# The first superblock's second product from seven products of halves, list-scheduled, with the low parts of w_out kept in SBUF

## The chip, the cores and the metric

The kernel runs on one core of a Trainium2 chip. The metric is the device time of one execution in microseconds. Engines are named as in the profile: PE (TensorE), PEld (its weight loads), DVE (VectorE), ACT (ScalarE), POOL (GpSimd), SP (SyncE, whose queue issues nearly all DMAs).

## The reference

Attention within chunks of 64 tokens, and behind it a feed-forward layer with ELU, all in float32:

```
scores = q @ k.T / 8              # 8 batches, 8 heads, 576 tokens in 9 chunks, head size 64
x      = softmax(scores) @ v      # -> 4608 tokens x 512
g      = elu(x @ w_in)            # 512 -> 2048
out    = g @ w_out                # 2048 -> 512
```

## The kernel before

**Split operands.** A float32 operand is held as a high part in PE's fast 32-bit format and a low part, the rest. `three` (L425 to L434) makes a product of two such operands from three matmuls (high with high, high with low, low with high) of 128 x 128 weights against 512 columns. All these matmuls have line 434.

**Blocks.** The 4608 tokens are 9 blocks of 512. Three plain blocks come first: for each of 16 slices f of the hidden layer, `hidden` makes h (12 matmuls), `elu` turns it into g, split into ghi and glo, and the second product adds g times w_out to four banks o0 to o3 (12 matmuls per f). `queue` holds the second products; they run one or two slices behind, and when the third block ends, 24 of these matmuls (f = 14 and 15) are left over.

**Superblocks.** The other six blocks are three pairs, "superblock" 0, 1 and 2. Two blocks are taken as a 2 x 2 arrangement of halves, and seven products of half size take the place of eight (`PRODUCTS`, `FIRST`, `SECOND`), with sums and differences of the operands made beforehand. A product over two blocks is 384 matmuls in the plain form and 336 in that of seven products.

- *First product.* The sums of w_in (`combine`) are made by POOL during the second block and written to `a_dram`. The sums of x ("t1" to "t4") and their splits ("B11", "T2" and so on, `prepare`) are made as soon as the tiles of x are there.
- *Second product.* Its operands come from w_out: `Sums` takes a pair j of slices (there are 8 pairs), adds high and low part ("a", "b"), makes four differences ("c", "d"), casts the high part on ACT ("e"), makes the low part ("f") and writes four halves to `w_dram` ("g" to "j"); `write_raw` writes the parts that need no sum.
- *Superblocks 1 and 2* have both products in this form. `superblock` and `tokens` put every step with its reads, writes and a place in time into a `Plan`; `Plan.order` lists them with a table of costs per engine, which sets the order on each engine. First operands and w_out operands come through a ring of four places of 512 KB in SBUF, tile `ring` (`ring_slot`, `load_entry`), one entry for two steps of six matmuls each.
- *Superblock 0* has the first product of seven, written out by hand (`FIRST_PAIR`, `SECOND_PAIR`, `PAIR`): one pair g of hidden slices at a time, its seven operands loaded by `load_a` into the former place of w_in. Its second product is plain: one block beside the first products, the other from g kept in SBUF (`KEPT`). Since x operands take the place of w_out's low part, that low part is written to `lo_dram` in the first block (`write_lo`) and read back through a ring of four (`load_lo`).

**Attention.** A tile is 128 tokens. Its queries and keys are loaded as tokens, transposed on DVE, multiplied (`score`, L248), turned into probabilities, transposed in 32 x 32 blocks, copied by ACT (`unturned`, L393), swapped by four DMAs on SP's queue (`turned`, L399), and multiplied by v (`times_v`, L256). The softmax has two forms: one subtraction and one ACTIVATE for all (L362, L367) in the hand-written stages, eight ACTIVATEs by head (L1566) in the planned ones.

**Order.** PE, ACT, DVE and SP run in the order in which the program is written, up to the third block also POOL by the framework's order; strings such as `THIRD_BLOCK` are lists of items, one per instruction group. Each engine works its queue in order, so a waiting instruction holds what stands behind it.

## Time and profile before

| | |
|---|---|
| time, 3 runs | 829.26, 825.13, 828.77 us; median 828.77 |
| the profiled execution | 825.15 us, span 823.4 us |
| busy, share of the span | PE 98%, PEld 80%, DVE 74%, ACT 64%, POOL 21% |
| DMA | 191.90 MB, mean 233 GB/s |
| third block ends, superblock 0 begins | 319.3 us |
| superblock 1 begins | 499.4 us |
| superblock 2 begins | 665.0 us |

The page cuts the span in 40 slices and gives busy tenths per engine; the chain of waits follows the last instruction back to what released it. A matmul's duration in the timeline (0.39 us) is longer than the distance to the next (0.23 us), because matmuls overlap.

### The profile page before, as it was taken

How to read it: one execution, taken by the hardware profiler on the slowest of the kernel's cores; microseconds unless marked ns; L12 is line 12 of the kernel's file. 1: busy time of each engine (PE TensorE's matmuls, PEld its weight loads, DVE VectorE, ACT ScalarE, POOL GpSimd, SP SyncE). 2: the span in 40 equal slices, each digit the busy share in tenths (PEclk: the TensorE clock that was granted, in tenths of full speed). 3: DMA queues.
4: the chain of work that ended last, by engine and by line, in shares of the span. 5: the costliest groups of instructions: out<-in, count | busy, mean ns of one | idle time of the engine just before them, and what ended most of it. 6: DMA issues, size and time to landing. Idle time of an engine off the chain costs nothing.

```text
span 823.4 us, 15851 instructions
## 1 busy us (share of the span) xinstructions
PE 804.4 (98%) x5853; PEld 655.6 (80%) x5853; DVE 613.1 (74%) x914; ACT 523.5 (64%) x990; POOL 171.1 (21%) x149
## 2 busy tenths in 40 slices
PE   6799999999999999999999999999999999999997
PEld 5688878888778878878888888778788888888885
DVE  4999997666776659767656867868889956557964
ACT  5999885544554546766666445888867737776451
POOL 0000014264525531443111254000020100000100
PEclk9999999999999999999999999999999999999999
DMA  9976994889778887689986789999876585566755
GB/s 234 272 212 209 270 328 130 244 243 267 219 215 231 231 269 205 202 241 281 283 235 188 218 246 299 286 322 287 249 204 206 195 269 193 193 196 190 226 186 149
DMA packets 183229, 191.90 MB, mean 233 GB/s; under 512 B 84720, under 2 KB 151792, under 8 KB 183152
## 3 DMA queue, kind: packets, MB, share of 16 engines
q1 hardware_dynamic: 182512, 188.80, 77.2%
q0 software_dynamic: 640, 2.10, 0.6%
q8 instruction: 46, 0.75, 0.4%
q14 instruction: 31, 0.25, 0.1%
HBM read 144.18 MB, written 42.99 MB: 227 GB/s over the span
## 4 chain that ended last, share of the span: by engine, by line
PE 83%; DMA 8%; SPq 3%; ACT 2%; DVE 2%; issue 1%; DVEq 0%; ACTq 0%
PE o L434 43%; PE h L434 34%; DMA ring<-a_dram 3%; PE ps_a L248 2%; PE ps_a L256 2%; SPq L206 2%; PE h L451 1%; DMA st<-in_moe_w_out_dram 1%; DMA kept<-in_k_dram 1%; DMA a_dram<-wi_lo 1%; DMA kept<-in_q_dram 1%; DMA a_dram<-wi_hi 1%; DMA v_sb<-in_v_dram 1%; PE ps_a L315 1%; DMA ring<-w_dram 1%
## 5 line engine op out<-in xcount | busy, mean ns | idle before, releaser
L434 PE MATMUL o<-wo_hi,ghi 128*128 128x512 f32 x272 | 107.6, 396 | 0.0
L434 PE MATMUL o<-wo_hi,glo 128*128 128x512 f32 x272 | 106.1, 390 | 0.3 <-DVE glo L479 0.3
L434 PE MATMUL o<-wo_lo,ghi 128*128 128x512 f32 x272 | 106.0, 390 | 0.0
L434 PE MATMUL h<-xhi,wi_hi 128*128 128x512 f32 x228 | 84.0, 397 | 0.1
L434 PE MATMUL h<-xlo,wi_hi 128*128 128x512 f32 x228 | 82.3, 390 | 0.0
L434 PE MATMUL h<-xhi,wi_lo 128*128 128x512 f32 x180 | 70.3, 390 | 0.0
L434 PEld LDWEIGHTS o<-wo_hi,glo 128*128 128x128 f32 x272 | 51.1, 188 | 11.7 <-DVE glo L479 0.7
L434 PEld LDWEIGHTS o<-wo_hi,ghi 128*128 128x128 f32 x272 | 51.0, 188 | 11.1
L434 PEld LDWEIGHTS o<-wo_lo,ghi 128*128 128x128 f32 x272 | 51.1, 188 | 10.2
L510 POOL TENSOR_TENSOR kept<-wi_hi,wi_lo 128x512 f32<-128x512 f32 x16 | 21.7, 1376 | 158.8 <-DVE xf L172 118.2
L471 DVE SCALAR_TENSOR_TENSOR e<-e,h 128x512 f32<-128x512 f32 x48 | 32.8, 684 | 25.2 <-ACT e L469 24.8
L434 PE MATMUL o<-split,ring 128*128 128x512 f32 x216 | 51.0, 390 | 0.0
L434 PEld LDWEIGHTS h<-xhi,wi_hi 128*128 128x128 f32 x228 | 42.6, 188 | 9.8 <-ACT kept L785 0.8
L434 PEld LDWEIGHTS h<-xlo,wi_hi 128*128 128x128 f32 x228 | 42.8, 188 | 8.5
L434 PEld LDWEIGHTS o<-split,ring 128*128 128x128 f32 x216 | 40.5, 188 | 8.4
L393 ACT COPY unturned<-turned 128x512 f32<-128x512 f32 x28 | 17.4, 621 | 46.0 <-DVE turned L388 37.9
L468 ACT ACTIVATE e<-h 128x512 f32<-128x512 f32 x48 | 28.6, 596 | 25.0 <-PE h L434 22.5
L476 ACT CAST ghi<-e 128x512 fp32r<-128x512 f32 x48 | 29.8, 621 | 19.8 <-DVE e L471 19.6
L746 POOL TENSOR_TENSOR glo<-e,ghi 128x512 fp32r<-128x512 f32 x16 | 20.7, 1296 | 96.9 <-ACT ghi L744 96.9
L434 PE MATMUL h<-split,ring 128*128 128x512 f32 x168 | 40.3, 391 | 0.0
L1492 ACT ACTIVATE e<-e 128x512 f32<-128x512 f32 x64 | 39.5, 630 | 1.0
L434 PEld LDWEIGHTS h<-xhi,wi_lo 128*128 128x128 f32 x180 | 33.8, 188 | 7.5 <-DVE wi_lo L185 0.4
(225 smaller groups left out, 2011.3 us busy)
## 6 DMA issues: line engine op xcount, KB each, us to landing
ring<-a_dram SPq DMA_DIRECT2D x56, 512.0 KB, 5.3
ring<-w_dram SPq DMA_DIRECT2D x56, 512.0 KB, 4.3
wi_hi<-a_dram SPq DMA_DIRECT2D x56, 256.0 KB, 5.3
kept<-in_q_dram SPq DMA_DIRECT2D x100, 128.0 KB, 3.8
kept<-in_k_dram SPq DMA_DIRECT2D x100, 128.0 KB, 4.0
wo_lo<-lo_dram SPq DMA_DIRECT2D x20, 512.0 KB, 5.8
v_sb<-in_v_dram SPq DMA_DIRECT2D x32, 256.0 KB, 5.4
st<-in_moe_w_in_dram SPq DMA_DIRECT2D x16, 512.0 KB, 4.9
```

The costliest lines, as they stand in the source:

```text
L206: nc.sync.dma_start(out=dst[p0:p0 + n], in_=src[b, :, s0:s0 + n, :].rearrange("h s d -> s h d"))
L248: nc.tensor.matmul(scores[halves[c], j, hp, :], lhsT=qT[halves[j], hp, halves[c]], rhs=kT[halves[j], hp, halves[c]], start=True, stop=True,)
L256: nc.tensor.matmul(x_ps[halves[j], c, hp, :], lhsT=v_sb[halves[c], 2 * hp + j, :], rhs=aT[halves[c], :, j * NK + hp], start=True, stop=True,)
L315: nc.tensor.matmul(turned_ps[half, h, :], lhsT=a[half, h, :], rhs=ident[half, half], start=True, stop=True,)
L393: nc.scalar.copy(out=unturned, in_=turned)
L434: nc.tensor.matmul(ps, lhsT=a, rhs=b, start=start, stop=stop, skip_group_check=onto)
L468: nc.scalar.activation(out=e, in_=h, func=AF.Relu, scale=-1.0)
L471: nc.vector.scalar_tensor_tensor(out=e, in0=e, scalar=-1.0, in1=h, op0=ALU.add, op1=ALU.max)
L476: nc.scalar.copy(out=ghi, in_=e)
L510: nc.gpsimd.tensor_tensor(out=out, in0=a, in1=b, op=op)
L746: engine.tensor_tensor(out=lo, in0=e, in1=hi.bitcast(F32), op=ALU.subtract)
L1492: nc.scalar.activation(out=units[u], in_=units[u], func=AF.Exp, scale=-1.0)
```

## The change

- Superblock 0 goes through the same plan as 1 and 2: `FIRST_PAIR`, `PAIR`, `KEPT`, class `Pair` and their helpers are gone, and `for s in range(NS)` takes the place of `range(1, NS)`. Its second product is also of seven products, 336 matmuls for 384.
- The 24 leftover matmuls of the third block are planned ahead of its first step (at -1 to -0.35), and so are the rest of the x sums and the softmax of the first tile (at -1.5), whose v product comes at step 5.
- The low parts of w_out stay in SBUF: `lo_dram`, `write_lo` and `load_lo` are gone; T1 and T2 take the place of the first half's low part, and g of pairs 4 and 5 that of the second half's.
- The sums of w_out are spread anew: pair 0 in the second block on DVE, 1 and 2 on POOL and 3 on DVE in the third block, 4 to 7 in superblock 0's first phase (`LATE_SUMS`, begun at steps 0, 8, 16 and 24). Before, 4 and 5 were made in the third block, 0, 3 and 1 in superblock 0, and 2, 6 and 7 in superblock 1.
- The raw parts are all written by the end of the second block; the ring's first four entries are loaded from slice 9 of the third block on ("R0" to "R3").

The core of the diff:

```diff
-            early_sums[j] = Sums(j, sums_place(j), [weights[j // 4 if preparing == "third" else 0][3][
-                :, (2 * j + i) % (NF // 2), :] for i in range(2)])
+            early_sums[j] = Sums(j, kept_st[2][:, :4 * TB] if j == 3 else flat(io), lows_of(j))
...
-            sums.write_half(lo, half, nc.gpsimd if preparing == "third" else nc.sync)
+            sums.write_half(*divmod("ghij".index(part), 2), nc.sync if j in SUMS_ON_VECTOR else nc.gpsimd)
+
+    def lows_of(j: int):
+        return [w_out_slices(2 * j + i)[1] for i in range(2)]
...
-        both = flat((weights[0][1], weights[1][3], xhi, xlo, *t3_place)[place])[...
+        both = flat((weights[0][1], weights[0][3], xhi, xlo, *t3_place)[place])[...
...
-        wlo = w_out_slices(f)[1] if plain else weights[0][3][:, f % (NF // 2), :]
+        whi, wlo = w_out_slices(f)
...
-        14: "l H e q e xT1a k e e xt3a xt2a xT2a xt4a P",
-        15: "H s v e x V e xt1b xt3b xT1b e xt2b e xT2b xt4b",
+        14: "l H e q e xT1a k e e xt3a P",
+        15: "H s v e x V e e e",
...
-    SUMS_ON_VECTOR = (1,)
-    RAW_SECOND = {3: (3, 1), 6: (4, 1), 9: (5, 1)}
+    SUMS_ON_VECTOR = (0, 3)
+    RAW_SECOND = {2: (3, 1), 4: (3, 0), 6: (4, 1), 8: (4, 0), 10: (5, 1), 12: (5, 0)}
+    MORE_SECOND = {
+        4: "w0a w0b", 8: "w0c w0d", 9: "w0e", 12: "w0f", 13: "w0g w0h", 14: "w0i w0j",
+    }
     MORE_THIRD = {
-        2: "w4a", 3: "w4b", 4: "w4c w4d", 5: "w4e w4f", 6: "w4g w5a", 7: "w4h w5b", 8: "w4i w5c w5d", 9: "w4j w5e",
-        10: "w5f", 11: "w5g", 12: "w5h", 13: "w5i", 14: "w5j",
+        2: "w1a", 3: "w1b", 4: "w1c w1d", 5: "w1e w1f w3a", 6: "w1g w3b", 7: "w1h w3c w3d", 8: "w1i w3e w3f",
+        9: "w1j R0 w3g w2a", 10: "w2b w3h", 11: "R1 w3i w2c w2d", 12: "w3j w2e", 13: "R2 w2f w2g", 14: "w2h", 15: "R3 w2i w2j",
     }
...
-    LATE_SUMS = (2, 0), (6, 8), (7, 22)
+    LATE_SUMS = (4, 0, 2), (5, 8, 6), (6, 16, 7), (7, 24, 6)
...
-    SCORES = (5, 18, 31, 44, 57, 70, 83, 97)
+    SCORES = (5, 18, 31, 44, 56, 69, 82, 95)
...
+    for m, (name, cols) in enumerate((("t2", "a"), ("T2", "a"), ("t1", "b"), ("T1", "b"), ("t4", "a"), ("t3", "b"),
+                                      ("t2", "b"), ("T2", "b"), ("t4", "b"))):
+        add_prepare(-1.9 + .2 * m, name, cols)
+    for m, name in enumerate(("T3", "T4", "B22")):
+        add_prepare(.5 + .3 * m, name, "ab")
+    first_n = (PLAIN + 2) * NTT
     later[first_n], later[first_n + 1] = attention.now, attention.following
-    later[first_n + 2] = attention.after
-    for s in range(1, NS):
+    if attention.after:
+        later[first_n + 2] = attention.after
+    add_softmax(-1.5, first_n)
+    add_turns(3.6, first_n + 1)
+    if first_n + 2 not in later:
+        add_load_qk(4.2, first_n + 2)
+    for s in range(NS):
         superblock(s)
```

How the order moves, at three places. On PE at the head of superblock 0, first before (behind the third block's last v product; `o` rows are second products of the third block, `h` rows the first pair of hidden slices):

```order
L256 MATMUL ps_a<-turned,v_sb 64x64 x16
L434 MATMUL h<-wi_lo,wi_hi 128x512 x6
L434 MATMUL o_2534<-wo_hi,ghi 128x512
L434 MATMUL o_2534<-wo_lo,ghi 128x512
L434 MATMUL o_2534<-wo_hi,glo 128x512
L434 MATMUL o_2535<-wo_hi,ghi 128x512
L434 MATMUL o_2535<-wo_lo,ghi 128x512
L434 MATMUL o_2535<-wo_hi,glo 128x512
```

and now, behind the 24 leftover products (rows of one step or of two equal ones; `ps_a` is an attention tile, scores and v product):

```order
L434 MATMUL h<-wi_lo,ring 128x512 x12
L434 MATMUL o_3697<-wi_lo,ring 128x512 x6
L434 MATMUL o_3713<-wi_lo,ring 128x512 x6
L434 MATMUL h<-wo_lo,ring 128x512 x12
L248 MATMUL ps_a<-k_turned,qT 64x64 x16
L256 MATMUL ps_a<-turned,v_sb 64x64 x16
L434 MATMUL o_3697<-wo_lo,ring 128x512 x6
L434 MATMUL o_3713<-wo_lo,ring 128x512 x6
```

The leftover products no longer alternate with the first products but stand ahead of them in one piece, and the first tile's v product stands six steps behind them.

On ACT at the same place, now (L658 casts an x operand, L1634 and L1240 copy a bank out of PSUM, L1338 and L1343 are the softmax by head, L393 the copy ahead of the swap):

```order
L1634 COPY g_kept<-o_2535 128x512
L658 CAST xlo<-xf 128x1024
L1338 ACTIVATE ps_a,z<-ps_a,mx 128x64 x8
L1343 ACTIVATE ps_a<-z 128x2x4
L658 CAST wo_lo<-xf 128x2x128
L1240 COPY kept<-h 128x512
L658 CAST t_place<-xf 128x1024
L1240 COPY kept<-h 128x512
L658 CAST xhi<-xf 128x1024
L1634 COPY g_kept<-o_2537 128x512
L393 COPY unturned<-turned 128x512
```

The copy ahead of the swap stands behind the softmax by head, four casts and four copies that wait for PE's leftover products and first steps. Before, the place had the casts and copies, and one ACTIVATE for the tile's softmax (L367).

On SP early in superblock 0, now (L1129 loads a ring entry, L596 writes half of a sum, L399 is the swap, L227 and L206 load tokens):

```order
L596 DMA w_dram<-g_kept 128x2x256
L1129 DMA ring<-a_dram 128x1024
L227 DMA kept<-in_k_dram 32x4x256 x4
L1129 DMA ring<-a_dram 128x1024
L596 DMA w_dram<-g_kept 128x2x256
L206 DMA v_sb<-in_v_dram 64x8x64 x2
L1129 DMA ring<-a_dram 128x1024
L399 DMA turned<-unturned 32x256 x4
L1129 DMA ring<-a_dram 128x1024
L596 DMA w_dram<-g_kept 128x2x256
```

Ring loads, writes of sums, token loads and the swap share one queue, as they did in superblock 1 before; here they stand in superblock 0.

More of the change, by code (lines that the diff above doesn't have):

```diff
@@ L578, in whole @@
                 in1=self.lows[i].bitcast(F32), op=ALU.add)
-        def load(self):
-            half, f = divmod(2 * self.j, NF // 2)
-            to = self.place[:, 1].rearrange("p (i d) -> p i d", i=2)
-            self.lows = [to[:, i] for i in range(2)]
-            nc.sync.dma_start(out=to, in_=lo_dram[half, :, f * DM:(f + 2) * DM].rearrange("p (f d) -> p f d", f=2))
         def sum(self, t: int, engine=nc.gpsimd):
@@ L605, in write_half @@
                 in_=self.place[:, lo].rearrange("p (i d) -> p i d", i=4)[:, of])
-        def write(self):
-            for lo in range(2):
-                nc.sync.dma_start(
-                    out=w_dram[:4, self.j // 2, :, self.j % 2, lo, :].rearrange("i p w -> p i w"),
-                    in_=self.place[:, lo].rearrange("p (i d) -> p i d", i=4))
     early_sums = {}
@@ L695, in b_operand @@
                     "B22": (3, 0), "T3": (4, 0)}[name]
-        both = flat((weights[0][1], weights[1][3], xhi, xlo, *t3_place)[place])[:, i * 4 * TB:(i + 1) * 4 * TB].rearrange(
+        both = flat((weights[0][1], weights[0][3], xhi, xlo, *t3_place)[place])[:, i * 4 * TB:(i + 1) * 4 * TB].rearrange(
             "p (l k t) -> p l k t", l=2, t=TB)
@@ L729, in prepare @@
             x_sum(name, cols)
[L731 to L793 removed]
+    queue = []
     def second(f, hi, lo):
@@ L1251 @@
     ps_a = ctx.enter_context(tc.tile_pool(name="ps_a", bufs=1, space=bass.MemoryType.PSUM))
-    run, following = (TB, o_tiles(), None), later[2 * NTT].steps()
+    run, following = (TB, o_tiles()), later[2 * NTT].steps()
     for f in range(NF):
@@ L1371 @@
     spare = late.tile([P, 2, TB], F32, name="spare")
-    c11, c21 = [spare[:, i] for i in range(2)]
     kept = [kept_st[2][:, i * TB:(i + 1) * TB] for i in range(4)]
@@ L1870, with add_sums @@
                      lambda tt=tt, place=place: nc.sync.dma_start(
-                         out=out[n0 + TB + tt * P:n0 + TB + (tt + 1) * P, :], in_=place),
+                         out=out[(PLAIN - 1) * TB + tt * P:(PLAIN - 1) * TB + (tt + 1) * P, :], in_=place),
                      [("G", 3, tt)], [])
-    def add_sums(t: float, j: int):
-        made, early = {}, j < NG // 2
-        g = 2 if early else 6 + j % 2
-        def begin():
-            to = flat(g_kept[:, 4 * g:4 * g + 4]) if early else g_more_of(g)
-            made[0] = Sums(j, to, [weights[0][3][:, (2 * j + i) % (NF // 2), :] for i in range(2)])
-        def load():
-            begin()
-            made[0].load()
+    def add_sums(j: int, t: float, g: int):
+        made = {}
         def whole(engine):
             if not made:
-                begin()
+                made[0] = Sums(j, flat(g_kept[:, 4 * g:4 * g + 4]) if g < 4 else g_more_of(g), lows_of(j))
             made[0].whole(0, engine)
@@ L1891, in add_sums @@
         raw = [("s", i, l) for i in range(4) for l in range(2)] + [
-            ("G", i, b) for i in ((6, 7) if early else (4, 5)) for b in range(4)]
+            ("G", i, b) for i in (4, 5) for b in range(4)]
         half = {"DVE": (350, 423), "POOL": (700, 740)}
-        if early:
-            plan.add(t - .9, "SP", dma(1, 1500), load, [], place[2:])
-        plan.add(t + .1, None, EITHER, whole, raw + place[2:], place[:1])
-        plan.add(t + .15, None, EITHER, lambda engine: made[0].whole(1, engine), raw + place[2:], place[1:2])
+        begin = [("step", t)]
+        plan.add(t + .1, None, EITHER, whole, raw + begin, place[:1])
+        plan.add(t + .15, None, EITHER, lambda engine: made[0].whole(1, engine), raw + begin, place[1:2])
         for i, (k, reads) in enumerate(((1, ()), (3, ()), (2, (("t", j, 1),)), (4, (("t", j, 2),)))):
             plan.add(t + .2 + .1 * i, None, half, lambda engine, k=k: made[0].sum(k, engine),
-                     [*place[:2], *reads], [("t", j, k)] + (place[2:] if k == 1 else []))
+                     [*place[:2], *reads], [("t", j, k), *place[2:]])
         plan.add(t + .7, "ACT", (955, 1047), lambda: made[0].high(),
```

204 lines of the change are left out of this document (17 added, 187 removed), and 39 rows, old and new, of tables (FIRST_BLOCK, KEPT, MORE_PAIR, THIRD_BLOCK).

## The prediction

> **What bounds the kernel now.** I read the page first (busy shares, the 40 slices, the chain of waits), then the chain in order of time, then PE's timeline at the places where the stages meet, and the list of PE's waits.
>
> ```profile
> PE 804.4 (98%) x5853; PEld 655.6 (80%) x5853; DVE 613.1 (74%) x914; ACT 523.5 (64%) x990; POOL 171.1 (21%) x149
> PEclk9999999999999999999999999999999999999999
> PE 83%; DMA 8%; SPq 3%; ACT 2%; DVE 2%; issue 1%; DVEq 0%; ACTq 0%
> 785.01 10.88 PE o L434 x48
> ```
>
> A busy PE is not yet a PE at its peak, so I look for the spacing. The last row gives it: 48 products of 512 columns in 10.88 us, 0.2267 us each, and PE is 83% of the chain. The clock is full in every slice. PE's timeline shows where superblocks 0, 1 and 2 begin (the first three rows) and the very last product; the first row is the old stage, the rest list-scheduled:
>
> ```profile
> 319.33 0.97 PE L434 MATMUL h<-wi_lo,wi_hi 128*128 128x512 f32 x3
> 499.44 0.84 PE L434 MATMUL h<-wi_lo,ring 128*128 128x512 f32 x3
> 664.99 0.39 PE L434 MATMUL h<-wi_lo,ring 128*128 128x512 f32 x1
> 817.90 0.39 PE L434 MATMUL o<-xhi,ring 128*128 128x512 f32 x1
> 446.48 1.52 PE L434 MATMUL h<-xlo,wi_hi 128*128 128x512 f32 x6
> 449.02 0.50 PE L434 MATMUL o<-wo_hi,ghi 128*128 128x512 f32 x1
> 449.36 0.39 PE L434 MATMUL o<-wo_lo,ghi 128*128 128x512 f32 x1
> ```
>
> Between the last three rows lies one attention tile: the six products from 446.48 end their slots at 447.84, the next begins at 449.02 and itself takes 0.34 instead of 0.23, so a tile costs PE 1.29 us. With that the stages can be set against their ideal:
>
> - superblock 0: 180.11 us. It runs 336 + 384 products and the 24 left over from the third block, 744 x 0.2267 = 168.66; eight tiles 10.32; lost 1.1.
> - superblock 1: 165.55 us, 672 x 0.2267 = 152.34 and 10.32; lost 2.9.
> - superblock 2: to 818.13, 153.14 us for 152.34 and no tiles; lost 0.8.
>
> So what a stage costs is its number of products, in the old form and in the list-scheduled one. Of the 2.9 us in superblock 1 the list of PE's waits names nearly half, three of them in that stage's first 45 us:
>
> ```profile
> PE o L434 <- DMA ring<-a_dram: 1.3, 3, 0.6
> ```
>
> **What the change removes.** Superblock 0's second product goes from 384 products to 336: 48 fewer, 48 x 0.2267 = 10.88 us of the bound engine. This is the one large term, **-10.9 us**. The sixteen writes and twenty loads of the low parts and the 56 loads of single first operands leave SP's queue, 56 ring loads of 512 KB enter it. In bytes: 4.2 + 10.5 + 14.7 MB out, 29.4 MB in, so the total stays. In the first block the low-part writes go while PE had no wait for any of them; that part I cost at nothing.
>
> **What it moves in the plain blocks.** The sums of pair 0 (second block) and pair 3 (third block) are made on DVE, those of 1 and 2 take the places of 4 and 5 on POOL. On DVE one pair's sums are two of 512 columns (0.68), four of 256 (0.42) and one of 1024 (1.22), about 4.3 us; on ACT one cast of 1.04.
>
> ```profile
> 160.00:180.00 20.00, 20.00 (x148) 16.39 (x148) 14.82 (x18) 8.65 (x14) 14.03 (x13) 1.00 0.93 281
> 260.00:280.00 20.00, 20.00 (x148) 16.35 (x147) 14.09 (x22) 9.70 (x16) 14.07 (x15) 1.00 0.84 238
> L576 DVE TENSOR_TENSOR g_more<-wo_hi,wo_lo 128x512 f32<-128x512 f32 x4 | 2.7, 681 | 0.0
> L591 DVE TENSOR_TENSOR g_kept<-g_kept 128x256 f32<-128x256 f32 x3 | 1.1, 417 | 0.0
> L597 DVE TENSOR_TENSOR g_kept<-g_kept 128x1024 fp32r<-128x1024 f32 x1 | 1.2, 1217 | 0.0
> L594 ACT CAST g_more<-g_more 128x1024 fp32r<-128x1024 f32 x2 | 2.1, 1044 | 0.2 <-POOL g_more L591 0.2
> ```
>
> These are 20 us stretches of the second and the third block (PE, PEld, DVE, ACT, POOL, clock, DMA): DVE idles 5 to 6 us in each of the two, and a block has four, so 4.3 us lie beside PE, and the queue of second products holds two rows (24 products, 5.4 us) of cover before a late low part reaches PE. Without that cover the cost is at most the 4.3 us per block; I take 0.
>
> **The head of superblock 0.** Here is the term that speaks against the change. Before, the first attention tile of this stage was multiplied by v a good 30 us in. Now the list puts it after the 24 leftover products and six steps. From 319.33: 24 x 0.2267 = 5.44, 36 x 0.2267 = 8.16, the scores of the next tile 0.5, so PE wants it at **333.5**. Its chain (maximum, exponentials, normalising, transposing, swapping) starts only when the third block's scores are there, and on ACT it stands in one queue with the casts of the operands and the copies out of PSUM. Rows for it:
>
> ```profile
> 318.24 0.69 PE L248 MATMUL ps_a<-k_turned,qT 64*64 64x64 f32 x32
> 318.76 0.65 PE L256 MATMUL ps_a<-turned,v_sb 64*64 64x64 f32 x32
> 322.71 0.41 ACT L711 CAST wo_lo<-xf 128x256 fp32r<-128x256 f32 x1 [1.19 <-DVE xf L720]
> 324.41 0.59 ACT L785 COPY kept<-h 128x512 f32<-128x512 f32 x1
> 324.89 1.05 ACT L711 CAST t_place<-xf 128x1024 fp32r<-128x1024 f32 x1
> 325.84 0.59 ACT L484 COPY g_kept<-o 128x512 f32<-128x512 f32 x1
> 512.70 0.28 ACT L1566 ACTIVATE ps_a<-ps_a,mx 128x64 f32<-128x64 f32 x1
> 516.19 0.18 ACT L1571 ACTIVATE ps_a<-z 128x8 f32<-128x8 f32 x1
> turned<-unturned SPq DMA_DIRECT2D x112, 32.0 KB, 2.4
> 251.81 1.85 SPq L399 DMA_DIRECT2D turned<-unturned  x3
> 301.52 0.58 SPq L399
> 302.15 4.23 DMA turned<-unturned
> 306.52 0.69 PE ps_a L256 x30
> ```
>
> ACT's starts give 0.48 us for a copy and 0.95 for a cast of 1024; the eight exponentials by head take 512.70 to 516.37, 3.67 us (the stage before used one ACTIVATE of 0.59 for all). In the new order the copy of the first leftover bank waits for 15 products after 319.33, to 322.9. Then: copy 0.5, cast 0.95, exponentials 3.67 (to 328.0), small cast 0.41, and copy, cast, copy, cast, copy 3.34 (to 331.8), the copy before the swap 0.62: 332.4. The swap is four DMAs; the last three rows show one that PE waited for: third issue at 301.52, landing 4.23 us after 302.15. With a landing of 2.4 us, the median of 112, behind 1.85 us for three issues it takes 4.3; with 4.23 in place of 2.4 it takes 6.1. I take 5.0, near the middle: 337.4. PE stands still for 337.4 - 333.5 = **+3.9 us**. Bounds: 0 if the queue is reached earlier than I walk it; 6.0 with the slow swap (5.0) and POOL 1.0 slower, since POOL makes the first two x sums there and its speed beside a busy DVE was
>
> ```profile
> L591 POOL TENSOR_TENSOR g_more<-g_more 128x256 f32<-128x256 f32 x6 | 7.7, 1298 | 1.0 <-DVE g_more L591 1.0
> L591 POOL TENSOR_TENSOR io<-io 128x256 f32<-128x256 f32 x4 | 2.9, 743 | 0.1
> ```
>
> in superblock 1 and in the third block: 1.75 times. T2's low part, that step 4 needs at 330.2, comes out at about 330.0 by the same walk: no wait of its own, with 0.2 to spare.
>
> **The late sums.** Superblock 0's first phase gets four pairs of sums (0, 8, 16, 24 steps in) where superblock 1 had three, and superblock 1 gets none. The ring waits of 1.3 us move with them: 0 net, and a third of them, **+0.4**, for the fourth pair. From below 0 net gain is excluded only if superblock 1's waits stay; from above see the DMA rival. The list-scheduled form lost 2.9 - 1.3 = 1.6 us besides, the old one 1.1: another **+0.4** (0.5 rounded down, since the head's stall lets transfers catch up).
>
> **Sum.** -10.9 + 3.9 + 0.4 + 0.4 = -6.2 us. The profiled execution took 825.15 us (span 823.4), so 819.0. That execution is at the low end of the runs shown (825.13, 828.77, 829.26); from the median it would be 822.6. I say **820**, between the two.
>
> **Rivals.**
>
> 1. *The head is hidden* and superblock 1 loses its ring waits without superblock 0 gaining them: 825.15 - 10.9 - 0 to 1.3 = 813 to 814.3. For it: of 28 swaps PE waited for one,
>
> ```profile
> PE ps_a L256 <- DMA turned<-unturned: 0.3, 1, 0.3
> ```
>
> 0.3 us. Against: the walk above has 3.9 us to lose before that, and there was no early tile in the old stage. 0.17.
>
> 2. *DMA becomes the bound of the first phase.* In 30 steps (40.8 us) it needs 15 ring loads (7.9 MB), 16 writes of sums (4.2), 2.3 tiles at 1.31 MB (3.0) and four outputs (1.05): 16.1 MB. The same count for superblock 1 before is 15.6, and its stretches show what the queues gave (the first row is the busiest of all, in the first block):
>
> ```profile
> 100.00:120.00 20.00, 20.00 (x177) 15.93 (x176) 18.57 (x27) 16.50 (x27) 0.46 (x1) 1.00 1.00 332
> 500.00:520.00 20.00, 19.96 (x147) 16.05 (x145) 18.60 (x31) 15.35 (x38) 10.00 (x8) 1.00 0.90 264
> 520.00:540.00 20.00, 18.75 (x137) 14.52 (x138) 16.29 (x27) 17.84 (x45) 1.30 (x1) 1.00 1.02 310
> 540.00:560.00 20.00, 20.00 (x148) 16.38 (x147) 12.41 (x21) 15.43 (x40) 0.00 (x0) 1.00 0.99 310
> ```
>
> At 310 GB/s with all engines busy, 16.1 MB take 52 us, 11.2 too long: 825.15 - 10.9 + 11.2 + 0.4 = 826, no change to be measured. Against it: before, 15.6 MB should have cost 9.5 us by the same count and cost 1.3, because four entries are there beforehand and the tiles' loads give way. 0.15. The Trainium skill, "DMA: Bandwidth & Descriptors" (Where 436 GB/s comes from), puts the limit of one core's HBM share at about 358 GB/s; by that the stretch would be 4.2 us late, an estimate, and the kernel at 819. No stretch of 20 us here passed the first row's 332 GB/s, and no row shows 358.
>
> 3. *Slower: SP's queue holds the ring back.* One queue issues ring loads and the sums' writes, in order; a write waits there for its cast and its low part, and the next ring load stands behind it. A ring slot is free 3 entries x 12 x 0.2267 = 8.16 us before its data are due, and a load lands in
>
> ```profile
> ring<-a_dram SPq DMA_DIRECT2D x56, 512.0 KB, 5.3
> ```
>
> so from 2.9 us of delay on PE pays. If each of the 16 writes holds a load 1.2 us beyond that, 19.2 us: 825.15 - 10.9 + 19.2 = 833.5. Against: the order sets at most two writes before a ring load, and 12 such writes in superblock 1 came with three waits of at most 0.6. 0.07.
>
> **How the numbers follow.** Forecast (815 to 823) 0.58, head hidden 0.17, DMA 0.15, slower 0.07, 0.03 left for the unforeseen. The likeliest's own range is 815 to 823; reaching to both neighbours, with the spread of 4 us between runs, 8 in 10 is 813 to 827.5. Against the median of 828.77 a measurement tells 0.5%, 4.1 us: faster is below 824.6. Forecast and hidden head, and 0.04 of the rest, make 0.79; DMA and what is left 0.14; slower 0.07.
>
> **What would show it.** Products of 512 columns 3216 before, 3168 after. Superblock 0 from its first leftover product to the next superblock: 180.1 now, 174 by my sum (168.1 for products and tiles, 6 lost); 169 to 170 by rival 1, over 178 by rival 2. Superblock 1 from 165.6 to 164, superblock 2 the same 153. The list of PE's waits: one of 3 to 4 us, for the swap (turned<-unturned) ahead of the first tile; ring waits around 1.7 us, all in superblock 0. Wrong is the step on the head if that wait is below 1 us or if PE waits there for an operand; wrong is the cover in the plain blocks if superblock 0 begins more than 1 us later than 319.3; wrong is the first term if superblock 0 is not shortened.

## The result: slower by 0.9%

| | before | changed |
|---|---|---|
| median, us | 828.38 (825.13 to 829.26, 4 runs) | 835.27 (834.49 to 835.85, 4 runs) |
| profiled execution, us (its span) | 825.15 (823.4) | 834.49 (832.4) |

The ratio is 1.009, 95% interval 1.0061 to 1.0119. I had forecast 820. These rows of the changed kernel's page answer to the first ones of the prediction (busy times, and the shares of the chain):

```profile
PE 798.4 (96%) x5805; PEld 646.4 (78%) x5805; DVE 653.4 (79%) x986; ACT 557.3 (67%) x1159; POOL 152.7 (18%) x136
PE 62%; DMA 12%; DVE 9%; ACT 6%; SPq 6%; issue 3%; POOL 1%; DVEq 0%; ACTq 0%
```

PE is busy 6.0 us less and is 62% of the chain instead of 83%: it waits more than it saved. PE's timeline says where. The rows are the first leftover product, the first products of superblocks 1 and 2, and the very last product.

```profile
323.49 0.50 PE L434 MATMUL o<-wo_hi,ghi 128*128 128x512 f32 x1
510.68 2.88 PE L434 MATMUL h<-wi_lo,ring 128*128 128x512 f32 x12
673.38 2.88 PE L434 MATMUL h<-wi_lo,ring 128*128 128x512 f32 x12
826.12 0.39 PE L434 MATMUL o<-xhi,ring 128*128 128x512 f32 x1
```

Set against the prediction's rows (319.33, 499.44, 664.99, 817.90), in us:

| stage | before | predicted | changed | difference |
|---|---|---|---|---|
| up to the leftover products | 319.33 | 319.3 | 323.49 | +4.16 |
| superblock 0 | 180.11 | 174 | 187.19 | +7.08 |
| superblock 1 | 165.55 | 164 | 162.70 | -2.85 |
| superblock 2, and to the end of the run | 160.2 | the same | 161.1 | +0.95 |

The 48 products are gone, but superblock 0 got longer: its products and tiles are 168.1 us, so it lost 19.1 us where I had 6. To see where, I cut it at the score products of its tiles (L248). Superblock 1 has the same tiles between the same products and loses next to nothing (PE's list of waits is empty there), so its pieces are the measure; by it the losses add up to 18.5:

| piece of superblock 0 | without loss | changed | lost |
|---|---|---|---|
| leftover products to the 1st tile (339.51) | 13.69 | 16.02 | 2.3 |
| 1st to 5th tile (421.63): the first product | 74.93 | 82.12 | 7.2 |
| 5th to 8th tile (487.53): the second product | 57.00 | 65.90 | 8.9 |
| 8th tile to superblock 1 (510.68) | 23.04 | 23.15 | 0.1 |

PE's waits in the second half of the plain blocks (200 to 323.5 us), from the list of waits (engine, what it waited for; us in total, times, longest). Before the change the same stretch had 0.3 for a swap and 0.3 for a low part.

```profile
PE ps_a L256 <- DMA turned<-unturned: 2.1, 3, 1.7
PE ps_a L248 <- DVE k_turned L351: 1.1, 1, 1.1
PE o L434 <- DVE glo L479: 0.7, 1, 0.7
```

and in superblock 0 (323.5 to 510.7 us):

```profile
PE o L434 <- DMA ring<-w_dram: 2.8, 4, 1.2
PE ps_a L256 <- DMA turned<-unturned: 2.1, 2, 1.2
PE o L434 <- DMA ring<-a_dram: 2.1, 4, 0.9
PE o L434 <- ACT unturned L393: 1.7, 1, 1.7
PE h L434 <- DMA ring<-w_dram: 1.1, 1, 1.1
PE h L434 <- DVE wo_lo L662: 0.8, 1, 0.8
PE h L434 <- ACT kept L1240: 0.8, 1, 0.8
PE o L434 <- ACT ps_a L1338: 0.7, 1, 0.7
PE o L434 <- ACT kept L1240: 0.6, 1, 0.6
```

The ring's waits are 6.0 of these 12.7 us; in the second product they are 3.9, beside 2.4 for ScalarE (L393 and L1338). The transfers of superblock 0, before (319.3 to 499.4 us; below the sums, its loads of operands):

```profile
DMA packets 38085, 43.40 MB, mean 241 GB/s; under 512 B 12810, under 2 KB 28339, under 8 KB 38066
q1 hardware_dynamic: 38066, 43.16, 81.9%
wi_hi<-a_dram SPq DMA_DIRECT2D x49, 256.0 KB, 5.4
wo_lo<-lo_dram SPq DMA_DIRECT2D x14, 512.0 KB, 5.8
ring<-a_dram SPq DMA_DIRECT2D x4, 512.0 KB, 5.8
g_kept<-lo_dram SPq DMA_DIRECT2D x1, 512.0 KB, 8.4
```

changed (323.5 to 510.7 us):

```profile
DMA packets 39611, 50.16 MB, mean 268 GB/s; under 512 B 15897, under 2 KB 31925, under 8 KB 39591
q1 hardware_dynamic: 39440, 49.42, 93.0%
ring<-a_dram SPq DMA_DIRECT2D x28, 512.0 KB, 6.0
ring<-w_dram SPq DMA_DIRECT2D x28, 512.0 KB, 6.6
```

It moves 6.8 MB more, and the one hardware queue takes 93% of the 16 engines' time instead of 82%. Nearly all of it is operands: 56 ring loads are 29.4 MB, and the loads listed for the stage before are 22.8. The next two rows are stretches of the changed kernel (busy PE, PEld, DVE, ACT, POOL; granted clock, DMA share, GB/s): the second product of superblock 0, and that of superblock 1.

```profile
421.60:487.50 65.90, 59.60 (x427) 45.98 (x426) 58.21 (x92) 44.75 (x112) 9.74 (x7) 1.00 1.01 258
593.90:650.30 56.40, 56.40 (x425) 46.54 (x425) 52.15 (x89) 42.58 (x109) 6.04 (x4) 1.00 0.64 203
```

In the first all 16 DMA engines are busy all the time (share 1.01). A ring load lands there 7.0 us after its issue, in superblock 1's second product 3.4 (the next two rows: 421.6 to 487.5, and 577 to 667 us).

```profile
ring<-w_dram SPq DMA_DIRECT2D x20, 512.0 KB, 7.0
ring<-w_dram SPq DMA_DIRECT2D x28, 512.0 KB, 3.4
```

But VectorE is busy 58.2 of these 65.9 us too, so which of the two binds had to be tried.

### The profile page after: what moved, and what is told of

The parts are those of the page before. It is cut to its first block, busy times and chain, and to the rows that moved or that the text cites. A ratio compares the mean times of both kernels' runs of the same rounds, so it can differ in the third digit from the quotient of the medians.

```text
span 832.4 us, 15902 instructions
## 1 busy us (share of the span) xinstructions
PE 798.4 (96%) x5805; PEld 646.4 (78%) x5805; DVE 653.4 (79%) x986; ACT 557.3 (67%) x1159; POOL 152.7 (18%) x136
## 2 busy tenths in 40 slices
DMA packets 185198, 191.38 MB, mean 230 GB/s; under 512 B 92448, under 2 KB 159520, under 8 KB 185120
## 4 chain that ended last, share of the span: by engine, by line
PE 62%; DMA 12%; DVE 9%; ACT 6%; SPq 6%; issue 3%; POOL 1%; DVEq 0%; ACTq 0%
PE o L434 36%; PE h L434 22%; DMA ring<-w_dram 3%; SPq L227 2%; DMA kept<-in_k_dram 2%; SPq L399 2%; SPq L206 2%; PE ps_a L248 1%; PE ps_a L256 1%; DMA a_dram<-kept 1%; DMA v_sb<-in_v_dram 1%; DMA turned<-unturned 1%; DVE kept L541 1%; DMA out_dram<-g_kept 1%; PE h L451 1%
## 5 line engine op out<-in xcount | busy, mean ns | idle before, releaser
L434 PE MATMUL o<-wo_hi,ghi 128*128 128x512 f32 x192 | 76.5, 399 | 0.0
L434 PE MATMUL o<-wo_hi,glo 128*128 128x512 f32 x192 | 75.2, 392 | 0.7 <-DVE glo L479 0.7
L434 PE MATMUL o<-wo_lo,ghi 128*128 128x512 f32 x192 | 74.9, 390 | 0.0
L1264 ACT ACTIVATE e<-e 128x512 f32<-128x512 f32 x96 | 59.2, 631 | 1.6
L434 PE MATMUL o<-ghi,ring 128*128 128x512 f32 x164 | 54.3, 391 | 2.4 <-ACT unturned L393 1.7
L434 PEld LDWEIGHTS h<-split,ring 128*128 128x128 f32 x252 | 47.1, 188 | 10.1 <-issue 0.2
L434 PE MATMUL o<-wo_lo,ring 128*128 128x512 f32 x216 | 52.0, 393 | 0.7 <-DMA ring<-a_dram 0.7
L434 PE MATMUL o<-wi_lo,ring 128*128 128x512 f32 x216 | 52.0, 392 | 0.4 <-DMA ring<-a_dram 0.3
L471 DVE SCALAR_TENSOR_TENSOR e<-e,h 128x512 f32<-128x512 f32 x48 | 32.8, 683 | 23.4 <-ACT e L469 23.3
L434 PEld LDWEIGHTS o<-wo_lo,ring 128*128 128x128 f32 x216 | 40.1, 188 | 9.9 <-issue 0.8
L434 PEld LDWEIGHTS o<-wi_lo,ring 128*128 128x128 f32 x216 | 40.1, 188 | 9.8 <-PE h L434 0.7
L1338 ACT ACTIVATE ps_a<-ps_a,mx 128x64 f32<-128x64 f32 x128 | 36.9, 288 | 11.4 <-DVE mx L1323 7.8
L393 ACT COPY unturned<-turned 128x512 f32<-128x512 f32 x28 | 17.4, 620 | 40.2 <-DVE turned L388 40.2
```

What stands on the lines that cost most here:

```text
L393: nc.scalar.copy(out=unturned, in_=turned)
L434: nc.tensor.matmul(ps, lhsT=a, rhs=b, start=start, stop=stop, skip_group_check=onto)
L471: nc.vector.scalar_tensor_tensor(out=e, in0=e, scalar=-1.0, in1=h, op0=ALU.add, op1=ALU.max)
L1264: nc.scalar.activation(out=units[u], in_=units[u], func=AF.Exp, scale=-1.0)
L1338: nc.scalar.activation(out=later[n].scores[:, j, h, :], in_=later[n].scores[:, j, h, :], func=AF.Exp, scale=SCALE, bias=mx[1][:, j, h, :], ...
```

## The experiments

Each is an edit of the changed kernel. The table has all of them (us): begin of the leftover products, the four pieces, superblock 0 in all, MB moved in it, what PE lost from 130 us to the end of superblock 0 at a granted clock below 1 (summed from 2 us stretches), and the run.

| run | begin | to 1st tile | 1st-5th | 5th-8th | to end | sb 0 | MB | clock | run |
|---|---|---|---|---|---|---|---|---|---|
| changed kernel | 323.5 | 16.0 | 82.1 | 65.9 | 23.2 | 187.2 | 50.2 | 0 | 834.5 |
| e_half_ring | 326.0 | 16.0 | 81.8 | 57.5 | 25.4 | 180.7 | 42.7 | 3.4 | 830.5 |
| e_no_sum_writes | 327.2 | 16.1 | 83.5 | 58.8 | 23.0 | 181.4 | 45.9 | 3.3 | 832.4 |
| e_fewer_sums | 324.9 | 16.2 | 81.5 | 65.7 | 23.0 | 186.4 | 50.2 | 3.4 | 835.0 |
| e_half_tokens | 324.1 | 16.1 | 82.3 | 57.0 | 25.2 | 180.6 | 45.2 | 1.7 | 829.0 |
| e_no_late | 326.0 | 16.0 | 80.6 | 57.4 | 24.2 | 178.2 | 45.9 | 3.4 | 827.3 |
| e_head_no_late | 324.3 | 17.4 | 77.7 | 59.2 | 25.0 | 179.3 | 45.8 | 0 | 829.0 |
| e_plain | 325.6 | 15.9 | 84.5 | 64.2 | 23.0 | 187.5 | 50.8 | 5.1 | 837.4 |
| e_w3_later | 325.4 | 16.7 | 81.4 | 63.2 | 23.2 | 184.5 | 50.4 | 1.7 | 834.2 |
| e_plain2 | 324.2 | 16.1 | 80.2 | 63.4 | 23.3 | 183.0 | 50.4 | 0 | 831.7 |
| e_plain2_head | 321.5 | 17.7 | 80.1 | 60.5 | 25.8 | 184.1 | 50.0 | 0 | 830.2 |
| e_five | 324.1 | 17.8 | 81.4 | 60.6 | 23.0 | 182.8 | 49.9 | 0 | 831.4 |
| e_five2 | 324.1 | 16.3 | 86.7 | 59.6 | 23.0 | 185.5 | 50.0 | 6.8 | 833.5 |
| e_five2_head | 325.4 | 22.0 | 76.1 | 63.6 | 24.8 | 186.5 | 49.5 | 1.7 | 837.1 |
| e_plain3_head | 320.6 | 18.5 | 79.8 | 64.0 | 24.6 | 186.8 | 49.6 | 0 | 832.8 (median of 5) |

With the first tile two steps later (the names with "head") 2.7 us pass from the second piece to the first. All but the last are one run each, and the last, run five times, spread from 829.68 to 836.0: differences of a few us between runs say nothing alone, so I read the pieces. The column "begin" has a spread of its own: a tile of the second block, ahead of every edit, begins between 133.4 and 136.1 us. The pieces too are of one trace for each kernel.

### The second product: DMA engines or VectorE?

**Half of each ring load.**

`raw_e` is the entry's number as it comes in; the line that keeps it isn't shown.

```diff
+        if phase and raw_e < ENTRIES:     # superblock 0's second product
+            nc.sync.dma_start(out=slot[:, :, 0].bitcast(F32), in_=of[:, :, 0])
+            return
         nc.sync.dma_start(out=slot.bitcast(F32), in_=of)
```

> In superblock 0's second product each of the 28 ring loads brings only the high half (256 KB for 512 KB); the low half of the slot keeps what was there, so this part of the output isn't computed. Same number of loads, same matmuls, same work on the other engines. In the changed kernel superblock 0 takes 187.2 us from the first leftover product to superblock 1's first product, 24.5 of them after the tile at 463.6; superblock 1 takes 162.7. Theory D (the 16 DMA engines are the bound of superblock 0: 50.2 MB at a share of 0.94): 7.3 MB less at the 271 GB/s of this stretch is 27 us of the engines' time, so the second product's losses (3.4, 0.6 and 5.0 us between the tiles at 421.6, 444.0, 463.6 and 487.5, against the same tiles of superblock 1) go, the loads land in under 5 us instead of 6.9, superblock 0 takes 177 to 180 us and the run about 826. Theory E (VectorE and ScalarE are late in the second product: VectorE busy 19.98 of 20 us at 444 to 464): nothing of this changes, superblock 0 takes 186 to 188 us and the run 834 to 836.

Measured: the second product takes 57.5 us, 0.5 from no loss, and PE's waits for its ring loads are 0.2 us in all, 3.9 before the edit:

```profile
423.70:481.20 57.50, 57.33 (x427) 46.59 (x426) 53.34 (x86) 41.10 (x108) 10.76 (x7) 1.00 0.79 203
```

VectorE has the same instructions as in the changed kernel, and they are as long: a split's low part takes 732 ns on average in this stretch, 734 in the changed kernel. This is theory D. Superblock 0 took 180.7 us (177 to 180 expected): 1.7 were lost at the fallen clock in its head, and PE waited 2.1 us for a low part on VectorE (row below) just before its end, so it met a second bound behind the first. Of the 4.5 us by which the run misses 826, 2.5 are the later begin of the leftover products.

```profile
502.61 0.50 PE L434 MATMUL o<-glo,ring 128*128 128x512 f32 x1 [2.10 <-DVE glo L1532]
```

**The late sums' writes left out.**

```diff
-        for i in range(4):
+        for i in range(0):
             plan.add(t + .9 + .5 * i, "SP", dma(1, 800), lambda i=i: made[0].write_half(i // 2, i % 2),
...
```

In the part not shown, the ring loads of the second products read the first four pairs' places and no longer wait for the sums. The last is a second change beside the bytes; in e_half_ring and e_half_tokens the ring loads still wait for the sums.

> The 16 writes of the four late pairs' sums (256 KB each, 4.2 MB in the first product of superblock 0) are left out, their arithmetic stays; the second products read the first four pairs' sums in their place, so half of that product's weights aren't the right ones. Theory D (DMA engines): 4.2 MB at the 268 GB/s of superblock 0 are 15.6 us of the engines' time; the first product's losses behind the ring (about 3 us) go and part of the second product's 9, because the queue enters it without a backlog: superblock 0 takes 176 to 181 us, the run 824 to 829. Theory E (the sums' arithmetic holds VectorE and ScalarE): superblock 0 stays at 186 to 188 us. If only the first product gains (2 to 4 us), the backlog isn't carried over.

Superblock 0 took 181.4, 0.4 above D's range and far from E's, but the gain isn't where I had put it: the bytes went from the first product, which gained nothing (83.5, of which 1.7 lost at the fallen clock), and the second gained 7.1 us. What the first product moves less, the second one no longer has ahead of it in the queue.

**Half of the late sums' arithmetic left out, all writes kept.**

```diff
-        add_sums(j, t, g)
+        (add_sums if j < 6 else add_writes)(*(j, t, g)[:3 if j < 6 else 2])
```

`add_writes`, which isn't shown, plans the four writes of a pair alone.

> The arithmetic of the last two late pairs (16 operations on VectorE or GpSimd and 2 on ScalarE) is left out, and all their 8 writes stay, with the second late pair's values, so these two pairs' weights aren't the right ones. Theory D: the same bytes, so superblock 0 takes 186 to 188 us and the run 834 to 836. Theory E: some 8 us less on VectorE and 2 on ScalarE in a stretch where they are busy 0.92 to 0.95 of the time, so the losses between the tiles at 362.7, 384.0 and 403.9 (3.1 us) go and superblock 0 takes 182 to 184 us, the run about 831.

VectorE is busy 153.8 instead of 160.3 us in superblock 0, which took 186.4, as theory D has it. Between the second and the fourth tile 1.6 us were gained, 0.9 lost again before the fifth, and the second product is what it was, 65.7 us. The operations left out stand in the first product: in the second, VectorE has 93 operations here and 92 in the changed kernel, so this run doesn't try VectorE there. It says that VectorE's work of the first product isn't carried over, as the bytes are.

**Half of the tokens.**

```diff
-            for piece in range(4):
+            for piece in range(2 if t < 4 * 7 * PAIRS else 4):
                 plan.add(t, "SP", dma(count, 460), lambda i=i, piece=piece: load(i, piece), [],
```

> Of each tile of q and k that is loaded in superblock 0 for the next one, two of the four pieces a side are left out (each tile's heads come twice, at two offsets; the second copy is left out, 5.2 MB and 40 issues of SP), so these tiles' scores aren't the right ones; every other instruction stays. Theory D (DMA bytes set superblock 0): 5.2 MB at 268 GB/s are 19 us of the engines' time, spread over both products, so every wait for a ring load goes and superblock 0 falls to its 168.1 us of products plus the head's 4 to 5 and a little behind VectorE: 173 to 178 us, the smallest of all runs so far (180.7 with 7.3 MB less in the second product alone, 181.4 with 4.2 MB less in the first), the share of the DMA engines to 0.85 to 0.9. Theory W (the second product waits for the late sums to be written, or the ring's four slots are too few): the waits for ring loads stay and superblock 0 takes 184 us or more.

The second product is now without loss, 57.00 us:

```profile
422.50:479.50 57.00, 57.00 (x427) 46.76 (x426) 53.57 (x87) 41.13 (x107) 9.46 (x6) 1.00 0.74 232
```

But superblock 0 took 180.6 and not 173 to 178: the first product stayed at 82.3, of which 1.7 were lost at the fallen clock, and PE waited 1.4 us for VectorE near the end. So DMA bytes explain the second product, and not, or not alone, the first.

Since a stall in the first product lets transfers catch up for the second, the two pieces can also be added, less the clock's losses in them, and with 2.7 us more where the first tile is later. Without loss this is 131.9 us. The five runs that move 42.7 to 45.9 MB stand at 136.4 to 140.6 us, the ten that move 49.5 MB or more at 141.2 to 148.0: the two groups don't overlap, but the second has a spread of 7 us that the bytes don't explain.

### The first product: the late sums or the head?

**The late sums left out altogether,** arithmetic and writes.

```diff
-    for j, t, g in LATE_SUMS:
-        add_sums(j, t, g)
...
```

The ring loads are changed as in the run without the writes.

> All of the four late pairs' work is left out of superblock 0, arithmetic and writes (some 36 operations and 4.2 MB); the second products read the first four pairs' sums in their place, so half of that product's weights aren't the right ones. So far the first product, from the tile at 339.5 to the one at 421.6, took 81.5 to 83.5 us with the writes taken away, with half of the arithmetic taken away and with half of the tokens taken away (74.9 in superblock 1). Theory E1 (there it is the sums' operations, all four pairs, among the tiles' on VectorE and ScalarE): 76 to 78 us, the 2 of the first tile's swap being what is left. Theory H (the first product is late from its own head: the first tile's swap, the preparation of the operands and ScalarE's softmax by heads): 80 us or more. The second product, from there to the tile at 487.5: 57 to 58.5 us by theory D (65.9 now). Superblock 0 by E1 and D together: 172 to 176 us, by H and D 178 to 181.

The second product took 57.4 us, as theory D has it. The first took 80.6, which by the numbers is theory H, as are the 178.2 of superblock 0. But 1.7 us of it were lost at a fallen clock (last section), so I tried it again on the order in which PE doesn't stand long at the head (`starts[0] = 7` for the first tile's step 5, and the plain blocks of e_plain2).

> The four late pairs' arithmetic and writes left out again, now on the order with the first tile two steps later, in which PE doesn't stand long at the head and the granted clock stayed at 1.00 (without that, 1.7 us of this stretch were lost at a clock of 0.5 and hid what the sums cost). From the tile at 339.2 to the fourth after it: 80.1 us in the run with the late pairs, 72.2 if nothing is lost (318 products and 4 tiles, less two steps). Theory E1 (the sums set the first product's losses): 73 to 74.5. Theory H (tiles, operand preparation and ring in the head): 77 or more. Half of the second product's weights aren't the right ones in this run. Superblock 0: 171 to 174 us by E1, 176 to 179 by H.

Nothing was lost at the clock, and the first product took 77.7 us, against 80.1 with the sums: they cost 2.4 us of it, and the other 5.5 above the 72.2 without loss are something else. That is theory H, narrowly (77 or more); superblock 0 took 179.3, 0.3 above H's range. The stretch from the second to the third tile lost 3.1 us even here:

```profile
360.70:382.80 22.10, 20.12 (x143) 15.73 (x142) 15.82 (x25) 17.13 (x43) 1.30 (x1) 1.00 0.98 277
```

The DMA share is 0.98: without the sums the queues are still full there. Of the changed kernel's 7.2 us I can name 2.1 (the swap) and, carried over from this order, about 2.4 (the sums); the last 2.7 stay unexplained. PE's list has 2.1 us for ring loads and 0.6 for a copy in this stretch, but as the row of the changed kernel's first product shows, the queues are nearly full and VectorE and ScalarE are each busy 69 to 70 of 82 us, and no run parted them.

```profile
339.50:421.60 82.10, 77.16 (x563) 60.74 (x562) 69.35 (x109) 69.95 (x169) 13.30 (x12) 1.00 0.94 283
```

### The plain blocks

**Order: pair 3's sums later, raw writes to the third block, pair 0's sums earlier.**

```diff
-    RAW_SECOND = {2: (3, 1), 4: (3, 0), 6: (4, 1), 8: (4, 0), 10: (5, 1), 12: (5, 0)}
+    RAW_SECOND = {2: (3, 1), 5: (3, 0), 8: (4, 1)}
+    RAW_THIRD = {8: (4, 0), 12: (5, 1), 14: (5, 0)}
-        4: "w0a w0b", 8: "w0c w0d", 9: "w0e", 12: "w0f", 13: "w0g w0h", 14: "w0i w0j",
+        4: "w0a w0b", 6: "w0c w0d", 7: "w0e", 8: "w0f", 9: "w0g w0h", 10: "w0i w0j",
```

and in the third block w3a from row 5 to row 7, the rest behind it.

> Only the order in the plain blocks is changed: pair 3's sums on VectorE begin two rows later (after the write of its place by the combine has landed), three of the six raw writes go from the second block to the third, and pair 0's sums and writes end four rows earlier. Theory P (the 4.2 us that the plain blocks lost are three waits: the second block's late low part, a swap held behind SP's added writes, VectorE held for the place): the waits of 0.7, 1.9 and 1.1 us go, the leftover products begin at 319.3 to 320.5 instead of 323.5, and the run takes 830.5 to 832.5. Theory Q (the sums cost their 8 us on VectorE wherever they stand, because the rows have no room): the leftover products begin at 322.5 or later and the run takes 834 or more. Superblock 0 itself stays at 186 to 188 us by both.

This is a miss for theory P: the leftover products begin at 325.6, and the run takes 837.4, which are theory Q's numbers. The waits of 1.7 and 1.1 us are gone, but there is one of 1.4 at the last swap, and PE's timeline has two new ones, for ScalarE and VectorE, among the rows into which I had moved pair 0's sums:

```profile
181.62 0.50 PE L434 MATMUL o<-wo_hi,ghi 128*128 128x512 f32 x1 [1.19 <-ACT ghi L476]
182.78 0.50 PE L434 MATMUL o<-wo_hi,glo 128*128 128x512 f32 x1 [0.43 <-DVE glo L479]
```

**The same with pair 0's sums nearly on their old rows** (8 "w0c w0d", 9 "w0e", 10 "w0f", 11 "w0g w0h", 12 "w0i w0j"), the raw writes in rows 3, 7, 11 of the third block.

> Order in the plain blocks alone: pair 3's sums two rows later as in the run before with that change, three raw writes moved to the third block but early in it (rows 3, 7, 11), and pair 0's sums left on their rows up to the high part, with the low part and the writes only two rows earlier. Theory P: the stall of 3.5 us that pair 0's crowded rows made in the second block in that run is gone, and so is the 1.4 us before the last tile; the leftover products begin at 319.5 to 321.5, the run takes 830 to 833. Theory Q (VectorE's rows in the second block have no room for the pair's 8 us): they begin at 323 or later. Superblock 0 stays at 186 to 188 us by both, as DMA bytes are the same.

From the tile at 246.9 on the next three follow 12.20 us apart, as before the change (14.71, 13.35 and 12.35 in the changed kernel). But the begin is at 324.2, not before 321.5, so by the numbers this is theory Q again: the second block and a wait of 1.5 us at the last swap took the rest. (One pair's sums are 4.3 us of VectorE, as the prediction has it; the 8 us of Q are two pairs.) Superblock 0 took 183.0 with the same bytes, below what both theories said.

**Pair 3's sums alone two rows later.**

```diff
-        5: "w1e w1f w3a", 6: "w1g w3b", 7: "w1h w3c w3d", 8: "w1i w3e w3f", ...
+        5: "w1e w1f", 6: "w1g", 7: "w1h w3a", 8: "w1i w3b", 9: "... w3c w3d", ...
```

> One edit alone: pair 3's sums on VectorE two rows later, nothing else. Theory P splits the plain blocks' 4.2 us by place: the wait for k_turned (1.1 us) between the tiles at 259 and 272 goes, that interval falls from 13.35 (12.8 with a wait of 0.5 in other runs) to 12.2; the swap's wait of 1.7 to 2.4 us between the tiles at 245 and 259 stays, since SP's added writes in the second block stay (14.7 us, 16.6 where the clock falls to 0.5 behind it). Total 833 to 836.

It came as theory P expected: the interval with the wait for k_turned falls to 12.22, that with the swap stays (16.86, with a wait of 2.6 and 1.7 of clock behind it). The leftover products did not begin earlier for it: 325.4. So there are two causes. One is VectorE, which in the changed kernel stood at its first sum until the place's old content was written out (VectorE's timeline):

```profile
265.83 0.69 DVE L575 TENSOR_TENSOR kept<-wo_hi,wo_lo 128x512 f32<-128x512 f32 x1 [2.47 <-DMA a_dram<-kept]
```

The other is SP. Its queue before the change (the swap is L399, its data were ready at 239.64):

```profile
237.02 1.72 SPq L486 DMA_DIRECT2D out_dram<-io  x2
238.84 0.41 SPq L206 DMA_DIRECT2D v_sb<-in_v_dram  x1
239.66 2.47 SPq L399 DMA_DIRECT2D turned<-unturned  x4
```

and in the changed kernel (ready at 240.48):

```profile
240.38 2.12 SPq L486 DMA_DIRECT2D out_dram<-io  x4
242.59 0.69 SPq L206 DMA_DIRECT2D v_sb<-in_v_dram  x1
243.38 2.97 SPq L399 DMA_DIRECT2D turned<-unturned  x4
```

The swap is issued 2.9 us after its data; before the change it was issued at once. At the tile before, SP was late already: the swap was issued at 230.98, 2.0 us after its data, and at 228.01, at once, before the change. Three more raw writes and four of pair 0's sums stand ahead of it in the second block. That it is these writes is argued from the order; the two runs above that move some of them have no wait at this swap, but they move other things as well.

### Can it be made to pay?

**The first tile of superblock 0 two steps later** (`if not s: starts[0] = 7`), on e_plain2.

> The same, and superblock 0's first tile two product steps (2.7 us) later. If its swap's wait (2.1 us, 4.1 in one run) is lateness of the tile alone, it falls to under 0.5 and the first product's head costs 2 us less; by theory D (DMA bytes) superblock 0 as a whole gains less than 1 us of it, because the ring catches up later: 185.5 to 187.5 us. By a theory in which each stall stands for itself, superblock 0 takes 184 to 185.5 us.

PE's waits for swaps fell from 2.1 to 0.7 us, and nothing was gained: up to the fifth tile superblock 0 takes 97.8 us against 96.4 without the edit, in all 184.1 against 183.0. PE waited instead for a copy on ScalarE (2.0 us, at 389) and for a sum on VectorE (1.3, at 415). That stalls don't stand each for itself is as theory D has it; its range, 185.5 to 187.5, was missed, and 184.1 lies in that of the other theory, since both had been reckoned from the 187 of the changed kernel and not from 183.

**A fifth pair in the third block,** three late ones.

```diff
-    LATE_SUMS = (4, 0, 2), (5, 8, 6), (6, 16, 7), (7, 24, 6)
+    LATE_SUMS = (5, 0, 2), (6, 8, 6), (7, 16, 7)
+    12: "w2e w4a w4b", 13: "R2 w4c w4d ...", 14: "w2h w4e w4f", 15: "R3 ... w4g w4h w4i w4j",
```

> The order of the last but one, and a fifth pair's sums on VectorE in rows 12 to 15 of the third block, behind pair 3's in the same place (which begin one row earlier for it), so that superblock 0 makes three late pairs instead of four: 1.05 MB of writes and 9 operations less there. Theory D: 1.05 MB at 268 GB/s are 3.9 us, superblock 0 takes 182.5 to 184.5 us. The plain blocks pay for it on VectorE: 8 us in four rows of 20 us with 5 us idle and the preparation of the first products beside them, so the leftover products may begin 1 to 3 us later than in the run without. Run 828 to 832.

Superblock 0 took 182.8, in D's range but only 0.3 below e_plain2. The third block paid: its last three intervals are 12.93, 13.97 and 14.31 us. The next run has the fifth pair two rows earlier (10 to 14):

> Five pairs in the plain blocks as before with that change, but the fifth pair two rows earlier, in rows 10 to 14 of the third block, with pair 3's in rows 6 to 9. If the end of the third block was slowed by the fifth pair on VectorE in the last four rows (4.5 us lost between the last three tiles and 2.3 us of a wait at the first product), the leftover products begin 2 to 3 us earlier after the tile at 232 than in that run (91.5 us then; 88 to 89.5 now), and superblock 0 takes 180 to 183 us. Run 827 to 830.

This is a miss: the run took 833.5 and superblock 0 185.5; the plain part from the tile at 232 took 92.1 us, and 6.8 us were lost at the fallen clock behind two swaps and a copy. The next has the later first tile as well:

> The same with superblock 0's first tile two product steps later. The waits of the head go (4 us); by theory D they come back as waits for ring loads in the second product unless the bytes leave room: with three late pairs superblock 0 moves 49 MB, at 274 GB/s 179 us, so it takes 179 to 181.5 us. Run 825 to 829, by the least of all orders so far.

This is a miss as well, 837.1: PE waited 1.7 and 2.3 us for copies on ScalarE at the head.

**The best parts together,** run five times: pair 3 in rows 6 to 11, raw writes in rows 1, 3 and 5.

> The best order so far (sums later, three raw writes in the third block, first tile two steps later: 830.2 in one run) with pair 3's sums in rows 6 to 11, so that no write of theirs stands before the last tiles' swaps, and the raw writes in rows 1, 3 and 5. Theory P: the wait for the last swap of the third block (1.5 us) goes, the leftover products begin 89.5 to 90 us after the tile at 231 (91.1 in the run before; 88.0 in the kernel before the change); superblock 0 takes 181 to 183.5 us. Median 828 to 830.5: about the time of the kernel before, ratio 0.999 to 1.003. If the sums of the plain blocks cost their time wherever they stand, it stays at 830 or more.

The third block is mended: from the tile at 232 to the leftover products it takes 88.4 us (88.0 before the change). The second isn't: from its tile at 134 to the one at 232 are 98.6 us, against 96.5 before the change and 97.2 to 98.6 in the changed kernel and the runs that leave its second block as it is. Superblock 0 took 186.8, as in the changed kernel, with 49.6 MB, and superblock 1 took 165.0 (162.7). The ratio to the kernel before is 1.0083, 1.0047 to 1.0119, where I expected at most 1.003. No order that I tried beat the kernel before. Why superblock 0 with the same bytes takes 183 in some orders and 187 in others stays open; with one trace of each, it may also be the spread between runs of one kernel.

## Why the prediction was wrong

The profiled executions went from 825.15 to 834.49, +9.3 us where I had -6.2.

- **"This is the one large term, -10.9 us"**: right, PE has 5805 matmuls for 5853; 168.1 us of products and tiles are left in superblock 0.
- **"so the total stays"** (the bytes): true of the program (191.90 MB before, 191.38 now), wrong where it counts. This is the step that failed. Superblock 0 went from 43.4 to 50.2 MB: the 56 ring loads stand in it whole, but of what I set against them the sixteen writes (4.2 MB) were issued by 146 us, and seven first operands and six low parts (5.0 MB) were loaded ahead of it. I priced the list-scheduled form of this stage at +0.4 us; its second product alone lost 8.9. Three runs that take away 4.2 to 7.3 MB in three different ways each brought that piece from 65.9 to between 57.0 and 58.8 us. No run took away VectorE's work in that piece; the first of the three leaves it all in, with the same durations.
- **"I take 0"** (the cover in the plain blocks): wrong by 4.2 us. I looked at VectorE's idle time over 20 us, and not at what it or SP would stand behind: a place still being written out, and, as the order has it, seven more writes ahead of a swap. The bound that I gave, 4.3 us for each of the two blocks, held.
- **"+3.9 us"** (the head): the size came out near by luck, 4.4 us, and not by the mechanism alone. PE waited 2.1 us for the swap, which landed 19.2 us after the leftover products began (I had 18.1). The other 2.3 were lost ahead of it: 0.8 for a copy, and 0.8 for the low part that should have had 0.2 to spare. Those waits also made PE want the swap later. That PE waits there for an operand is the sign that I had named for this step being wrong.
- **The late sums**, "0 net" and "+0.4, for the fourth pair": I had 1.7 us for all four, 1.3 of them moved from superblock 1. They cost about 2.4 us in the first product (80.1 against 77.7), and 4.2 MB of the queue that the second product pays for.
- **"174 by my sum"** is not what the terms give: the 1.3 us of ring waits that leave superblock 1 belong into superblock 0, which makes 175.2. The sum for the run has them right.
- Superblock 1 took 162.7 us, nearly without loss; I had 164. Its waits for the ring, 1.3 us, were gone when the late sums had left it.
- **Rival 2** (the DMA engines) had the mechanism, with 0.15, and the wrong place: I counted the first 30 steps, and not the second product, which takes over the backlog. Beside it I had the 358 GB/s of the Trainium skill ("DMA: Bandwidth & Descriptors", Where 436 GB/s comes from), by which the stage would have room; the trace does not agree: in the second product the engines are full at 258 GB/s.
- **Rival 3** ended nearest, at 833.5, by another mechanism. SP's order and number of issues are the same in e_half_ring, and the waits went; so in superblock 0's second product it is the transfers and not SP's queue. In the plain blocks a late issue on SP's queue did cost a wait, at a swap.

## What to carry to other kernels

Count the bytes of each stage, not of the program, and set them against the rate that this mix reached with all engines full. Here a stage whose share rose from 0.82 to 0.93 had a product in it at 1.01, where PE paid 8.9 us; a transfer "takes the place of another" only if both stand in the same stage. Work put into idle time is free only if nothing in front of it in the queue makes it wait: look up what the place was used for last, and what stands behind the new instruction. Where a bound is shared over a stage, a stall mended ahead of it can come back behind it.

## What I had not expected of the chip

A wait of PE can cost more than its length. In e_half_ring PE waits 2.4 us for a swap until 248.8, and the granted clock (last column but two) falls behind it:

```profile
246.00:248.00 2.00, 0.41 (x28) 0.27 (x20) 0.17 (x1) 1.04 (x2) 2.00 (x2) 1.00 0.97 231
248.00:250.00 2.00, 0.91 (x23) 0.80 (x27) 0.00 (x0) 0.00 (x0) 1.74 (x2) 0.76 0.39 113
250.00:252.00 2.00, 2.00 (x25) 1.59 (x18) 0.76 (x2) 0.59 (x1) 0.00 (x0) 0.50 0.97 239
252.00:254.00 2.00, 2.00 (x9) 1.61 (x8) 1.88 (x3) 1.15 (x2) 0.05 (x1) 0.89 0.57 145
```

The loss is (0.24 + 0.50 + 0.11) x 2 = 1.7 us, as much as 3.4 us at half speed. The same 1.7 us, once or twice over, came in nine of the fourteen runs from 130 us on, at one to three places where PE had waited 1.6 to 4.1 us; 14 of the 16 places are swaps. (In the first 35 us, where PE waits for its first loads, the clock falls in every profile but that of the kernel before.) It doesn't always come: the changed kernel's profile has a wait of 2.1 us at 341 without it, e_no_late has the same wait with it. Away from the tiles, five waits of 2.0 to 2.3 us left the clock at 1.00, and one of 2.5 us did not. The Trainium skill, "TensorE: Matmul & The Clock Gate" (Part 1), says that the clock halves after an idle window of about 3.4 us, and that the windows run freely; the length and the chance of it agree with these rows, but PE was never idle for 3.4 us here: it seems that the wait and the tile's 64 x 64 products around it were enough, which no run tried by itself.
